# A causal linear attention feeding a snake feed-forward layer on one core: a rebuilt head, another planner, shifted preferences

## The chip, the core and the metric

The kernel runs on one core of a Trainium2 chip. A core has a matrix engine (PE; its weight loads are shown apart as PEld), a vector engine (DVE), a scalar engine (ACT), a general engine (POOL) and a queue engine (SP) that issues most transfers. Each takes its instructions in order and waits on semaphores. PE multiplies tiles of up to 128 x 128 weights by up to 512 columns and writes into eight accumulator banks; DVE and ACT read these banks, POOL does not. Transfers issued by SP, ACT and POOL are moved by the same 16 DMA engines.

The metric is the device time of one execution in microseconds (us); less is better. The profile is one execution taken by the hardware profiler, and its span runs from the first to the last recorded instruction.

## The reference, cut to what matters

```python
for b in range(nb):                    # 12 blocks of 64 positions; B=4, H=8, S=768, D=64
    intra = einsum('bhic,bhjc->bhij', qb, kb) * Dmask      # lam**(i-j) for i >= j
    intra = einsum('bhij,bhjd->bhid', intra, vb)
    inter = einsum('bhid,bhde->bhie', qb * lam_pow, kv_state)
    out[:, :, sl] = intra + inter
    kv_state = lam_block * kv_state + einsum('bhsd,bhse->bhde', kb * rev_pow, vb)
x = out.transpose(0, 2, 1, 3).reshape(3072, 512)
h = x @ w_in                           # 512 x 2048
g = h + sin(alpha * h)**2 / (alpha + 1e-09)
return g @ w_out                       # 2048 x 512
```

An attention whose weights decay by lam per position, then a feed-forward layer with the function h + sin^2(alpha h)/alpha.

## The kernel before, in words

**Tiling.** The kernel takes 24 blocks of 128 positions (6 per batch entry, numbered s = 0 to 23) and groups four of them into a chunk of 512 rows, six chunks in all. Per block, `scale_block` multiplies q by powers of lam and k by inverse powers (POOL, some on DVE in the first four blocks) and casts v (ACT or POOL). `piece_T`, `piece_Q` and `piece_K` transpose the scaled q and k through PE for blocks below 12 (a DMA transpose does it from block 12 on) and copy the result into `qkT`. `part_S` multiplies k by q into two banks; DVE multiplies them by the mask into `Sm` (L646). `part_Z` adds k times v into bank 7, the running state, which is copied into `Zd` (block diagonal, L681) or `Zc` (L686). `part_O` adds the part from the state (`Zd` or `Zc` times q, L708 or L721) and the part within the block (v times `Sm`, L730) in one bank, and its `then` copies that bank, transposed x, into `xT` (L740).

Per chunk c and slice m of 128 of the 2048 hidden columns, `unit_A` multiplies w_in by `xT` (4 matmuls of 512 columns, L779), ACT takes the sine (L789), POOL or ACT squares it (L794 or L793), DVE forms `gT` from it and the bank (L796). `unit_A2` does two slices for half a chunk (8 matmuls of 256 columns, L813; L823, L827 or L828, L831). `unit_B` multiplies `gT` by w_out for 128 rows and four slices (4 matmuls, L844); after four of them ACT copies the bank into `osb` (L857) and it is stored (L859).

**The first four blocks (the head).** q of blocks 0 to 3 is loaded so that a partition holds four neighbouring positions, so a bank of outputs holds, for each t of 4, the positions 4x+t; the copy at L740 writes them in natural order, with a step of four elements of two bytes. Before its first real work PE multiplies a constant tile (`spin`, L935). A column block of 512 of w_in is loaded as f32 into `ws` and cast by DVE (L415); the rest of w_in and all of w_out are loaded with a cast by POOL's queue.

**What sets the order.** The program lists operations with what they read and write; `_Plan` orders them. It keeps a clock per engine, takes a duration from each `op` call, and places the operation that can start first; where several can start within a slack the one listed first goes (minus its `lead`). ACT, DVE and POOL operations are free in order, and an operation with a list of engines goes to the one that would end it first by these costs. PE may look 40 operations ahead, SP stays in listed order. Transfers are planned as an issue, a fixed 0.8 us, their duration shared among queues, and a latency. The result is a fixed instruction order with semaphore waits; the chip does not choose again.

```python
    AHEAD = {"PE": 40, "SP": 1}
    SLACK = 0.3
    LAT = 0.2
```

Of the kernel before, what the change touches and what calls it, by code (L numbers as in the profile page):

```python
# [32 lines left out]
class _Plan:  # L33

    AHEAD = {"PE": 40, "SP": 1}
    SLACK = 0.3  # L40
    EARLY = 0.0, 0.0

    LAT = 0.2
# [10 lines left out]
    def op(self, eng, emit, dur, reads=(), writes=(), dma=None, after=(), issue=0.4, lat=2.6, runs=64):  # L54
# [14 lines left out]
        o.deps.discard(o)  # L69
        o.lead = self.lead  # L70
# [4 lines left out]
    def _transfers(order):  # L75
# [5 lines left out]
        left = {e: [[o.start + 0.8, o.runs, o.dur / o.runs, o] for o in sorted(q, key=lambda o: o.start)]  # L81
# [19 lines left out]
    def _settle(self):  # L101

        filler, lands, best = self.filler, {}, None
        for _ in range(8):
            self.filler = filler
            for o in self.ops:
                o.eng, o.start, o.done = o.given, None, None
            order = self._order(lands)
            new = self._transfers(order)
            off = sum(abs(t - o.done) for o, t in new.items())  # L110
            state = [(o, o.eng, o.start, o.done) for o in order]
            if best is None or off < best[0]:
                best = off, order, state
# [5 lines left out]
    def _order(self, lands):  # L119
        index = {o: i - o.lead for i, o in enumerate(self.ops)}  # L120
        left = {}
        for o in self.ops:
            left.setdefault(o.eng if isinstance(o.eng, str) else "any", []).append(o)
        fixed = {e: left.pop(e, []) for e in ("PE", "SP")}
        free = [o for e in left for o in left[e]]
        clock = {e: 0.8 for e in ("PE", "SP", "ACT", "DVE", "POOL")}
        wire = 0.0
        port = 0.0
        order = []

        def ready(o):
            t = 0.0
            for d in o.deps:
                if d.done is None:
                    return None
                t = max(t, d.done + (0.0 if d.eng == o.eng else self.LAT))
            return t

        while fixed["PE"] or fixed["SP"] or free:
            best = None  # L140
            for e in ("PE", "SP"):
                can = []
                for o in fixed[e][:self.AHEAD[e]]:
                    r = ready(o)
                    if r is not None:
                        can.append((max(r, clock[e]), index[o], o, e, o.dur))
                if can:
                    soon = min(c[0] for c in can)
                    soon += self.EARLY[1] if e == "PE" and soon < self.EARLY[0] else self.SLACK
                    c = min((c for c in can if c[0] <= soon), key=lambda c: c[1])  # L150
                    if best is None or c[:2] < best[:2]:
                        best = c
            for o in free:
                r = ready(o)
                if r is None:
                    continue
                if o.port:
                    r = max(r, port)
                if isinstance(o.eng, str):
                    c = (max(r, clock[o.eng]), index[o], o, o.eng, o.dur)  # L160
                else:
                    _, e, d = min((max(r, clock[e]) + d + late, e, d) for e, d, late in o.eng)
# [81 lines left out]
def bass_lightning_attn__then__act_snake_kernel(  # L244
# [24 lines left out]
    R2 = 6  # L269
# [766 lines left out]
```

## Time and profile before

| | us |
|---|---|
| runs of the kernel before | 224.34, 221.33, 223.85; median 223.85 |
| profiled execution | 221.06, of which the span is 219.2 |
| PE busy | 207.6 (95% of the span) |
| ACT busy | 157.2 (72%) |
| DVE busy | 123.0 (56%) |
| POOL busy | 96.0 (44%) |
| first matmul of the feed-forward (L813) | starts at 20.58 |
| last matmul (L844) | ends at 216.6 |

Between the profiled execution's time and its span lie 1.86 us. A line of the timeline has the start in us, the duration in us, the engine (with q, its instruction queue), the line of the code, the operation, the tile written and the tile read, the shape and the number of instructions merged; in brackets the idle time of the engine just before and what ended it. A line of the chain of work that ended last has a start, a duration and what ran. A line of the waits has who waited for whom, the total in us, the number of times and the longest. PE durations include a modelled end, so that neighbouring ones overlap; starts are the better measure. Some matmul records are missing: where a group of four shows as x3 with 0.16 us of "issue" before it, the gap is one missing matmul.

### The profile page before, as it was taken

What the parts mean: (1) busy time and instruction counts of PE and PEld (TensorE: products, weight loads), DVE (VectorE), ACT (ScalarE), POOL (GpSimd) and SP (SyncE); (2) the same over time, 40 slices, a digit from 0 to 9 for tenths busy, and PEclk for the clock granted to TensorE, in tenths of its full rate; (3) what the DMA queues carried; (4) which work ended last, traced back from release to release, by engine and by line L of the source; (5) the groups of instructions that cost most, each with busy time, mean ns of one, the idle gap of its engine ahead of it and who ended that gap; (6) DMA issues with size and microseconds to landing.
All of it is one profiled execution on the core that took longest, in us unless ns stands there. A gap on an engine that the chain in (4) does not pass through costs nothing.

```text
span 219.2 us, 4238 instructions
## 1 busy us (share of the span) xinstructions
PE 207.6 (95%) x1714; PEld 112.2 (51%) x1739; DVE 123.0 (56%) x185; ACT 157.2 (72%) x279; POOL 96.0 (44%) x110
## 2 busy tenths in 40 slices
PE   7787999999999979999999999999999999999995
PEld 2365544446577656555445444545544444444454
DVE  4688675444878858957564556545464544444100
ACT  4577986364988888969798787878778677777221
POOL 7793677756886777574551533011001011110100
PEclk9999999999999999999999999999999999999999
DMA  4999999999999999999999560110011011101212
GB/s 132 310 314 210 207 215 214 220 219 250 235 314 221 240 186 271 162 290 179 281 254 208 123 144 10 41 48 35 16 48 51 0 48 48 51 0 48 87 58 96
DMA packets 78499, 33.31 MB, mean 152 GB/s; under 512 B 55296, under 2 KB 75536, under 8 KB 78480
## 3 DMA queue, kind: packets, MB, share of 16 engines
q1 hardware_dynamic: 71728, 24.25, 53.4%
q0 software_dynamic: 3696, 3.67, 10.1%
q10 hardware_dynamic: 3056, 5.13, 6.5%
q8 instruction: 13, 0.21, 0.4%
q14 instruction: 6, 0.05, 0.1%
HBM read 27.28 MB, written 6.29 MB: 153 GB/s over the span
## 4 chain that ended last, share of the span: by engine, by line
PE 66%; DMA 20%; POOL 5%; ACT 3%; DVE 2%; issue 2%; SPq 1%; ACTq 0%; POOLq 0%
PE bank L844 33%; PE bank L779 22%; DMA k<-in_k_dram 10%; PE bank L813 4%; DMA w<-in_moe_w_in_dram 4%; DMA q<-in_q_dram 3%; DMA v<-in_v_dram 3%; PE bank L730 2%; PE bank L635 2%; POOL qk L513 2%; SPq L346 1%; POOL u L794 1%; POOL qk L505 1%; PE bank L708 1%; DVE gT L831 1%
## 5 line engine op out<-in xcount | busy, mean ns | idle before, releaser
L844 PE MATMUL bank<-w,gT 128*128 128x512 bf16 (+1 forms) x382 | 91.3, 371 | 1.8 <-issue 1.3
L796 DVE SCALAR_TENSOR_TENSOR gT<-u,rinv,bank 128x512 bf16<-128x512 bf16 x74 | 54.6, 745 | 52.2 <-ACT u L793 30.0
L779 PE MATMUL bank<-xT,w 128*128 128x512 bf16 x290 | 73.1, 379 | 0.6 <-issue 0.2
L789 ACT ACTIVATE t<-bank,alpha 128x512 bf16<-128x512 f32 x74 | 50.5, 686 | 23.2 <-PE bank L779 23.1
L794 POOL TENSOR_TENSOR u<-t 128x512 bf16<-128x512 bf16 x26 | 26.9, 1039 | 86.6 <-ACT t L789 84.7
L844 PEld LDWEIGHTS bank<-w,gT 128*128 128x128 bf16 x400 | 37.9, 98 | 39.5
L779 PEld LDWEIGHTS bank<-xT,w 128*128 128x128 bf16 x296 | 28.5, 98 | 34.1 <-ACT xT L740 0.6
L646 DVE TENSOR_TENSOR Sm<-bank,mask 128x1024 bf16<-128x1024 f32 x24 | 29.1, 1222 | 10.4 <-PE bank L671 7.1
L793 ACT ACTIVATE u<-t 128x512 bf16<-128x512 bf16 x48 | 30.0, 628 | 1.3
L857 ACT COPY osb<-bank 128x512 f32<-128x512 f32 (+1 forms) x25 | 14.2, 571 | 14.3 <-PE bank L844 14.2
L505 POOL TENSOR_TENSOR qk<-q,Lq 128x512 bf16<-128x512 f32 x20 | 20.4, 1042 | 8.2 <-DMA q<-in_q_dram 8.2
L813 PE MATMUL bank<-xT,w 128*128 128x256 bf16 x176 | 22.5, 273 | 1.5 <-DVE gT L831 1.5
L525 POOL TENSOR_TENSOR qk<-k,Lk 128x512 bf16<-128x512 f32 x20 | 20.8, 1042 | 2.6 <-DMA k<-in_k_dram 2.5
L823 ACT ACTIVATE t<-bank,alpha 128x256 bf16<-128x256 f32 x44 | 18.5, 474 | 4.5 <-PE bank L813 4.1
L831 DVE SCALAR_TENSOR_TENSOR gT<-u,rinv,bank 128x256 bf16<-128x256 bf16 x44 | 18.8, 474 | 4.9 <-ACT u L827 2.6
L813 PEld LDWEIGHTS bank<-xT,w 128*128 128x128 bf16 x176 | 16.1, 98 | 4.8 <-DVE gT L831 2.4
L740 ACT CAST xT<-bank 128x512 bf16<-128x512 f32 (+1 forms) x18 | 14.4, 799 | 3.6 <-PE bank L671 2.2
L528 ACT CAST v<-v 128x512 bf16<-128x512 f32 x16 | 9.8, 614 | 4.3 <-DMA v<-in_v_dram 4.3
L828 POOL TENSOR_TENSOR u<-t 128x512 bf16<-128x512 bf16 x9 | 9.3, 1038 | 6.5 <-ACT t L823 6.5
L730 PE MATMUL bank<-Sm,v 128*64 128x128 bf16 (+1 forms) x224 | 11.0, 224 | 0.6 <-DVE Sm L646 0.3
L635 PE MATMUL bank<-qkT 64*128 64x128 bf16 (+1 forms) x224 | 9.6, 219 | 0.3 <-ACT qkT L594 0.2
L935 PE MATMUL bank<-idle 128*128 128x512 bf16 x21 | 8.4, 540 | 1.6 <-DVE idle L441 1.5
(68 smaller groups left out, 125.7 us busy)
## 6 DMA issues: line engine op xcount, KB each, us to landing
q<-in_q_dram SPq DMA_DIRECT2D x12, 512.0 KB, 5.6
k<-in_k_dram SPq DMA_DIRECT2D x24, 256.0 KB, 5.5
v<-in_v_dram SPq DMA_DIRECT2D x24, 256.0 KB, 5.7
out_dram<-osb ACTq DMA_DIRECT2D x19, 256.0 KB, 2.0
w<-in_moe_w_out_dram POOLq DMA_DIRECT2D x4, 512.0 KB, 12.7
w<-in_moe_w_in_dram POOLq DMA_DIRECT2D x3, 512.0 KB, 8.0
ws<-in_moe_w_in_dram SPq DMA_DIRECT2D x2, 512.0 KB, 6.2
out_dram<-osb SPq DMA_DIRECT2D x4, 256.0 KB, 4.2
```

Of the source, the lines that this page charges most:

```text
L505: lambda e, a=a: e.tensor_tensor(qk2[:, j:j + 2, 4 * a:4 * a + 4, :], q32[:, jq, 4 * a:4 * a + 4, :, :].rearrange("p h t d -> p t h d"), b ...
L525: lambda e: e.tensor_tensor(qk2[:, j, H:2 * H, :], block32(k32, jl), lk, ALU.mult), 1.05,
L646: op("DVE", lambda e: e.tensor_tensor(Sm[js][:, :, :], banks[:, 512 * b0:512 * b0 + 1024].rearrange("p (c i) -> p c i", i=128), bass.AP(ma ...
L779: ins = e.matmul(ps[hb][:, c0:c1], w1[:, kc, 128 * m:128 * (m + 1)], xT[x][:, kc, c0:c1], start=(kc == 0 and c0 == lo), stop=(kc == NKC - ...
L789: op("ACT", lambda e: e.activation(t16[ju][:, w], ps[hb][:, w], ACTF.Sin, scale=alpha[:, m:m + 1]), 0.69 * f, [bank(hb), "alpha"], [("t16" ...
L793: lambda e: (e.activation(u16[ju][:, w], t16[ju][:, w], ACTF.Square) if e is nc.scalar else e.tensor_tensor(u16[ju][:, w], t16[ju][:, w], ...
L794: e.tensor_tensor(u16[ju][:, w], t16[ju][:, w], t16[ju][:, w], ALU.mult)), 0,
L796: op("DVE", lambda e: e.scalar_tensor_tensor(out=gT[g][:, m, w], in0=u16[ju][:, w], scalar=rinv[:, m:m + 1], in1=ps[hb][:, w], op0=ALU.mul ...
L813: ins = e.matmul(ps[hb][:, 256 * i:256 * i + 256], w1[:, kc, 128 * (m + i):128 * (m + i + 1)], xT[x][:, kc, lo:lo + 256], start=(kc == 0 a ...
L823: op("ACT", lambda e, i=i: e.activation(t16[ju][:, 256 * i:256 * i + 256], ps[hb][:, 256 * i:256 * i + 256], ACTF.Sin, scale=alpha[:, m + ...
L831: op("DVE", lambda e, i=i: e.scalar_tensor_tensor(out=gT[g][:, m + i, lo:lo + 256], in0=u16[ju][:, 256 * i:256 * i + 256], scalar=rinv[:, ...
L844: ins = e.matmul(ps[ob][:, w], gT[g][:, m, 128 * s4:128 * (s4 + 1)], w2[:, m, w], start=(m == 0), stop=(m == NM - 1),)
```

## The change

1. **Head, constants.** The decay rates `lam` are loaded by SP ahead of q instead of by ACT. An Exp of one element stands right behind the Ln. The copy of alpha moves to ACT, behind the load of the Sin table; the two small DVE operations on it are listed later.
2. **Head, scaling.** All four q operations and three of four k operations of blocks 0 to 3 go to DVE (before: two q and one k), the rest to POOL; they are marked so that the planner does not lay DVE's and POOL's over each other. v: one of four on ACT.
3. **Head, transposes and outputs.** `piece_Q` can use two banks, with one ACT copy for each half. `piece_P` computes the part within the block for two blocks at once, each 64 x 64 matmul in one of four quarters of the array (32 matmuls for two blocks; before 16 for each block in turn); `piece_I` adds the part from the state. `evict` copies to `xT` with a step of two elements instead of four, all but half of the last block on ACT.
4. **First rows.** The rows of chunk 0 are now in another order in `xT`, so each group of 128 rows goes out in two stores of 64 partitions (eight stores on SP instead of four).
5. **Planner.** Every engine may take the earliest in preference among the operations that can start within a window (0.3 us for PE, 0.1 for ACT, DVE and POOL). A clock is freed a little before an operation's result is ready (`PIPE`), a hand-over costs `HOP` (plus `DRAIN` behind PE), transfers start 2.0 us after their issue (2.9 for POOL). Durations are changed all over. SP follows preferences too.
6. **Twelve shifts.** `MOVES` adds to the preference of stretches of operations.
7. The filler matmuls have 256 columns instead of 512.

In the built program ACT has 82 squares (before 61) and POOL 14 (before 35); ACT has 24 copies to `Zd` (before 19), DVE 2 (before 7). The counts of feed-forward matmuls are equal. SP loads k of one of blocks 4 and 5 ahead of q of the pair; on POOL's queue the first two loads of w_out stand ahead of the last load of w_in.

```diff
-    AHEAD = {"PE": 40, "SP": 1}
-    SLACK = 0.3
-    EARLY = 0.0, 0.0
-    LAT = 0.2
+    AHEAD = 40
+    WINDOW = {"PE": 0.3, "ACT": 0.1, "DVE": 0.1, "POOL": 0.1}
+    PIPE = {"ACT": 0.11, "DVE": 0.09, "POOL": 0.045, "PE": 0.0}
+    HOP = {"PE": 0.055, "ACT": 0.035, "DVE": 0.035, "POOL": 0.075, "SP": 0.1}
+    DRAIN = 0.085
+    MOVES = (
+        (112, 1, "SP", -15), (532, 3, "SP", -15), (291, 1, "all", 20), (104, 1, "all", 35),
+        (194, 30, "all", 35), (255, 10, "all", 50), (315, 1, "all", -110), (349, 30, "DVE", 125),
+        (487, 1, "all", -25), (80, 30, "all", -5), (328, 10, "SP", -20), (346, 3, "DVE", 740),
+    )
+    SPIN = 0.22, 0.11, 7.4
...
+        self.lag = 2.9 if eng == "POOL" else 2.0
...
     def _settle(self):
...
+        prio = {o: i - o.lead for i, o in enumerate(self.ops)}
+        for at, width, kind, by in self.MOVES:
+            for o in self.ops[at:at + width]:
+                if (kind == "all" and o.given != "SP") or o.given == kind or (kind == "any" and not isinstance(o.given, str)):
+                    prio[o] += by
...
+                soon = min(x[0] for x in c) + self.WINDOW.get(e, 0.0)
+                x = min((x for x in c if x[0] <= soon), key=lambda x: (x[1], num[x[2]]))
+                if best is None or x[0] < best[0]:
+                    best = x[0], x[2], e, x[3]
...
+                o.done = t + dur
+                clock[e] = o.done - self.PIPE[e]
...
-    QD = ((0, 0), (1, 0))
+    QD = ((0, 0), (0, 2), (1, 0), (1, 2))
...
-            load(lam_bc[:, :], bass.AP(lam.tensor, 0, [[0, 128], [1, H]]), "lam", 0.1, "lam", "ACT", runs=1)
+            load(lam_bc[:, :], bass.AP(lam.tensor, 0, [[0, 128], [1, H]]), "lam", 0.1, "lam", "SP", lat=0.8, runs=1)
...
+            op("ACT", lambda e: e.activation(warm[:, :], lnlam[:, 0:1], ACTF.Exp, scale=0.0), 1.5, ["lnlam"], ["warm"])
...
-            op("DVE", lambda e: e.tensor_copy(alpha[:, :], ps[4][:, 0:NM]), 0.2, [bank(4)], ["alpha"])
+            op("ACT", lambda e: e.copy(alpha[:, :], ps[4][:, 0:NM]), 0.2, [bank(4), "warm"], ["alpha"])
...
-                        eng, dur = (("DVE", 0.9) if a == 0 else ("POOL", 1.05)) if s == 0 else ("POOL", 1.05)
-                        (op(eng, lambda e, a=a: e.tensor_tensor(
+                        eng, dur = ("DVE", 0.68) if s + a < 3 else ("POOL", 1.05)
+                        ported(op(eng, lambda e, a=a: e.tensor_tensor(
...
+            def evict(s, obs):
+                jq, nq, u = queries(s)
+                c, i4 = s // BPC, s % BPC
+                P.lead = -20
+                for eng, a0, a1, dur in (("ACT", 0, 2, 0.46), ("DVE", 2, 4, 0.4)) if len(obs) > 1 else (("ACT", 0, 4, 0.74),):
+                    op(eng, lambda e, a0=a0, a1=a1: (e.copy if e is nc.scalar else e.tensor_copy)(
+                        xT[c % RX][:, a0:a1, BL * i4:BL * (i4 + 1)].rearrange("p a (u x t) -> p a u t x", u=nq // 2, t=2),
...
+            def piece_P(s, *obs):
...
+                    for t in range(2):
+                        for jp in range(4):
+                            for h in range(2):
+                                for i in range(2):
+                                    r = slice(64 * i, 64 * i + 64)
+                                    ins = e.matmul(
+                                        ps[obs[i][jp // 2]][64 * h:64 * h + 64, 128 * jp:128 * (jp + 1)],
+                                        v2[r, j + t, 2 * jp + h, :], Sm[sm[t]][r, 4 * h + jp, :],
...
+            def piece_I(s, *obs):
+                jq, nq, u = queries(s)
...
+                            Zd[(s - 1) % 2][:, jp, :], qkT[:, jq:jq + nq, jp, u],
...
-                    op(eng, lambda e: e.dma_start(out[row:row + 128, w], osb[jo][:, w]), 0.75,
-                       [("osb", jo)], [], dma=f"out{jo}", issue=0.3, runs=8)
+                    for u in range(1 if c else 2):
+                        rows = out[row:row + 128, w] if c else bass.AP(
+                            out.tensor, (row + 2 * u) * DM + lo, [[4 * DM, 32], [DM, 2], [1, hi - lo]])
+                        got = osb[jo][:, w] if c else osb[jo][64 * u:64 * u + 64, w]
...
             piece_S(2, 1, 2)
             piece_Z(0)
-            piece_O(0, 3)
             piece_S(3, 5, 6)
+            piece_P(0, 3, 4)
             piece_Z(1)
-            piece_O(1, 4)
+            piece_I(1, 4)
             piece_Z(2)
-            piece_O(2, 1)
-            piece_O(3, 2, 5)
+            piece_P(2, 1, (2, 5))
+            piece_I(2, 1)
+            piece_I(3, 2, 5)
...
-                    ins = e.matmul(ps[0][:, :], idle[:, 0:128], idle[:, :])
+                    ins = e.matmul(ps[0][:, 0:256], idle[:, 0:128], idle[:, :])
```

More of the change, by code (lines that the diff above doesn't have):

```diff
@@ L69, in op @@
         o.deps.discard(o)
+        if lag is not None:
+            o.lag = lag
         o.lead = self.lead
@@ L101, in _settle @@
     def _settle(self):
[L103 to L111, printed above, removed]
+        prio = {o: i - o.lead for i, o in enumerate(self.ops)}
[3 more added lines that the diff above has]
+                    prio[o] += by
+        lands, best = {}, None
+        for _ in range(10):
+            order, new, off = self._pass(prio, lands)
             if best is None or off < best[0]:
-                best = off, order, state
+                best = off, order, [(o, o.eng, o.start, o.done) for o in order]
+            if off < 0.5:
+                break
             lands = new
@@ L117, in _settle, with _pass @@
         return best[1]
[L119 to L121 removed]
+    def _pass(self, prio, lands):
         for o in self.ops:
[L123 to L168 removed]
@@ L194, in _order @@
             order.append(o)
+            can.discard(o)
+            left -= 1
+            for s in after.get(o, ()):
+                waits[s] -= 1
+                if not waits[s]:
+                    can.add(s)
         return order
@@ L595, in piece_K, with run @@
                        0.6, [bank(tbs[t])], [("kT", jt + t)])
-            def run(*parts, after=()):
+            def run(*parts, after=(), lead_then=-20):
                 parts = [p for p in parts if p is not None]
```

238 lines of the change are left out of this document (161 added, 77 removed).

## The prediction

> **What bounds the kernel now.** I read the page's slices first: PE is at 0.9 or more of its time in nearly all of the 40, and the matrix clock is granted in full throughout. So the time is the start of PE's real work, plus that work, plus its stalls. The timeline of the head shows when the work starts:
>
> ```profile
> 15.79 1.31 ACT L740 CAST xT<-bank 128x512 bf16<-128x512 f32 x1 [0.23 <-PE bank L730]
> 16.83 0.86 ACT L681 CAST Zd<-bank 64x256 bf16<-64x256 f32 x2
> 17.71 1.32 ACT L740 CAST xT<-bank 128x512 bf16<-128x512 f32 x1
> 18.77 0.86 ACT L681 CAST Zd<-bank 64x256 bf16<-64x256 f32 x2
> ...
> 20.58 2.02 PE L813 MATMUL bank<-xT,w 128*128 128x256 bf16 x16
> ...
> 22.65 1.68 PE L779 MATMUL bank<-xT,w 128*128 128x512 bf16 x7
> ```
>
> ACT alternates between copies of the state and of x without a pause; the last parts of xT come from it, and the first matmul of full width starts at 22.65. DVE is as full from 12.71: four Sm of 1.155 each, then the casts of ws:
>
> ```profile
> 9.52 1.52 DVE L513 TENSOR_TENSOR qk<-k,Lp 128x512 bf16<-128x512 f32 x1
> ...
> 12.71 4.62 DVE L646 TENSOR_TENSOR Sm<-bank,mask 128x1024 bf16<-128x1024 f32 x4 [0.53 <-PE bank L635]
> 17.24 1.79 DVE L415 CAST w<-ws 128x1024 bf16<-128x1024 f32 x2
> ```
>
> Then the waits of PE after the head, from the list of waits; "issue" entries are missing records, not waits:
>
> ```profile
> PE bank L813 <- DVE gT L831: 1.5, 2, 1.2
> ...
> PE bank L543 <- POOL qk L525: 0.5, 1, 0.5
> ```
>
> That is about 2.2 us with the small ones: all that a planner can win in the 196 us from 20.58 to the last matmul at 216.6. The chain of the work that ended last tells where the 0.48 (at 41.27) and the 1.20 (at 79.71) come from:
>
> ```profile
> 23.92 16.09 DMA k<-in_k_dram
> 40.08 1.05 POOL qk L525
> ...
> 71.40 6.17 DMA v<-in_v_dram
> 77.60 0.62 ACT v L528
> 78.21 0.54 ACT u L827
> 78.78 0.88 DVE gT L831 x2
> 79.71 1.05 PE bank L813 x8
> ```
>
> A load of k competes with the weights for 16 us; and an ACT queue stands behind a cast whose v has not landed, with the square that PE's bank needs behind it.
>
> **The head, step by step.** *Transfers.* lam ahead of q on SP costs one issue (0.46), so q starts at 1.27 instead of 0.81 and all that follows on that queue is 0.46 later. The second k landed at 9.19 (2.42 + 6.77); at some 290 GB/s a load of 262 KB takes 0.9, so the four k land at 8.7, 9.65, 10.55, 11.45, the four v at 12.35 to 15.05, and ws (10.13 + 6.0 and 11.0 + 6.5 before) at 16.6 and 18.0.
>
> *Constants.* lam took 3.5 from issue; at worst it lands at 4.3 again, at best with the 1.7 of a small store, 2.5. The dummy Exp saves nothing: the table load for Exp already started at 4.59, right behind the Ln, ahead of the DVE product at 4.61; it adds 0.2. Even with the late lam the factors are there at 6.2, and q lands at 1.27 + 5.0 (the shortest of its rows) = 6.3. Before, scaling began at 6.15: what is late next is q, so this step is worth nothing.
>
> *DVE.* Four q at 0.66: 6.3 to 8.95. k: to 9.6, 10.3; the small operation 0.6, to 10.9; third k to 11.6. Here I take 0.66, the row for q, not the 1.52 of the one k row, which ran beside POOL's k; only the third now meets POOL, so the bound is +0.85. Copy of k 0.42, reciprocal 0.25: Sm can begin at 12.3 and ends at 16.9 (before 17.33). The first cast of ws ends at 17.8.
>
> *POOL* has one k (11.45 to 12.5) and v to 13.85, then issues two weight loads until 15.5, fourth v to 16.1. The first weight load is issued at 13.85 instead of 13.45.
>
> *ACT.* k copies to 14.1, v 0.62 to 14.8. Then Zd 0.76, x, Zd 0.86, x, Zd 0.76, x and half an x. What is x worth? The step-4 copies took 1.31, half of one 0.73; later blocks with step 2 take 0.72 to 0.74 (L740 at 139.26, for one). I take 0.74 and 0.45: x ends at 16.3, 17.85, 19.4 and the half at 19.85. The matmuls hide beside it: the pair product waits for the last Sm (16.9) and the third state, runs 17.6 to 18.25 (before 0.47 of weight loads per 16, so 0.94 for 32 as an upper bound), the state part follows to 18.6, the last one to 19.05.
>
> [...]
>
> *Sum.* PE's first eight half-width matmuls 19.05 to 19.9, the next eight from 19.9 to 20.8 (second ws cast done at 20.55), first full-width matmul at 20.8 against 22.65: **1.85 won**. Bounds: 0.8, if DVE's k are slow and ws is held up by the earlier weight loads; 2.5, if lam's transfer hides and the Zd copies run at the 0.36 of the later rows.
>
> **From 20.8 to 42.** The loads do not move, as DMA is full from 4 to 40 us. k of the pair follows q as before, so the transpose that waited until 41.27 comes at about 41.6 (the weights start 0.4 later). But three more units of the output layer (3 x 0.863 = 2.6) are now ordered ahead of it, so PE reaches it at 20.8 + 0.44 + 14 x 0.863 + 9 x 0.863 + 0.45 = 41.55: the 1.85 is filled and the 0.48 goes. Net 2.6 - 0.3 = 2.3 ahead. Those units need the third load of w_out at about 38.5; it was issued at 24.57, and these loads took 12.7 (median) to 15.0, so it lands between 37.3 and 39.6: a wait of 0 to 1.1, I take 0.3 by the median. **2.0 won by 42.**
>
> **After 42.** Planned time to landing of a v goes from 4.5 (0.8 + 1.1 + 2.7) to 5.9 (2.0 + 1.18 + 2.7); the rows say 5.5 to 5.7, and 6.17 in the stall shown. Costs of ACT and DVE also move toward the rows (square 0.6 to 0.63 against 0.628). So I expect half of the 1.46 at L813 gone, **0.75**; bounds 1.46 and a loss (below). The eight stores instead of four hold SP longer (four took 2.83 from 59.39, so up to 2.8 more), and k and v of block 13 stand behind them. The cover: before, q of that pair was issued at 62.26, transposed from 73.09 on, and used by PE from 85.86, where a DMA transpose takes 5.4 to land: some 4 us to spare. I cost it at nothing; without that cover, up to 2. The tail (last matmul to end) stays at 2.6.
>
> **Sum.** 219.2 - 2.0 - 0.75 = 216.45, and with 1.86 around the span **218.3**, against the profiled 221.06 (-1.2%). The three runs have a median of 223.85, 1.3% above that execution: two executions lie near 221.2 (the profiled one with them), two near 224.1. The same two levels for the changed kernel would be 218.3 and 221.2. I forecast **219.4**, a third of the way up. About 2% is what a measurement of this kernel can tell from no change.
>
> **Rivals.**
> - *Everything works:* head 2.5 and all 2.2 of stalls gone: 214.5 + 1.86 = 216.4, 2.1% faster. For it: the costs match the rows now. Against: loads still decide at 40. Chance 0.20.
> - *The head's gain is waited away:* the third and fourth w_out loads, now behind another order, land a microsecond or two later (the fourth is issued only when the last of w_in, moved behind two others, has landed). PE waits at 38 to 42, and only the 0.75 stays: 218.45 + 1.86 = 220.3. Chance 0.16.
> - [...] Chance 0.10. [...]
> - *ACT becomes the bound (slower):* 21 squares move from POOL (1.04) to ACT (0.53 start to start before an independent one), with 5 Zd copies. From 86 to 130 ACT was busy 36.5 of 44, with 6 store issues of 0.34 besides; six to eight squares more and some copies make about 44. There is then no room, and each late v holds PE's banks as at 79.71, for 1.2. It decides from about six such waits on: 6 x 1.2 over the forecast, 225.5, 2% slower. Against: the new plan counts ACT's time closely, and POOL was open to it at a cost. Chance 0.10.
>
> The forecast's own case has 0.44. The range runs from 216.4 to 220.3 + 2.9 = 223.2; beyond it lie the slower case and an upper tail. Faster by over 2%: the first rival and a part of the forecast at its low level, 0.29; slower by over 2%: 0.09; within: 0.62.
>
> **What would show it.** x copies of 0.74 on ACT in the head; Sm from about 12.3; the first full-width L870 near 20.8; no wait of DVE on ACT above 1 us around 60 to 80; ACT near 172 us busy in all. Wrong if L870 starts after 22, if PE waits over 1 us for a w_out load near 38, or if PE's waits on DVE's gT grow past 2.

## The result, and the profile after

The changed kernel took 219.28 us (median of four runs, 218.18 to 221.55) against 222.97 for the kernel before beside it (four runs, 221.33 to 224.34): a ratio of 0.985, 95% interval 0.980 to 0.990. It is faster, by less than the 2% that separates a change from none. The ratio is of the means of all four runs; without the one of 221.55, which lies over 1.5% above the fastest and so counts as a slow run, it is 0.982. The forecast was 219.4, with a range of 216.4 to 223.2.

The profile after is of the slowest of the four runs: 221.55, with a span of 219.8, 0.6 longer than the span of before. One trace thus shows both what was won and where it was lost again. On its page, the slices of PE and of the granted clock:

```profile
PE   7788999999999998959999999999999999999995
...
PEclk9999999999999999979999999999999999999999
```

A slice is 5.5 us. In the 16th and the 18th (82 to 88 and 93 to 99) PE waits, and the 18th shows a clock of 0.7. Before, the slice with a wait was the 15th, and none showed a lower clock. The timeline of the head, for DVE, ACT and PE (start, busy time, engine and line, and in brackets the idle time ahead of it):

```profile
3.74 0.21 ACT L486 ACTIVATE lnlam<-lam_bc 128x8 f32<-128x8 f32 x1 [1.20 <-DMA lam_bc<-in_lam_dram]
3.96 1.28 ACT L488 ACT_TABLE_LOAD   x1
...
5.61 2.66 DVE L519 TENSOR_TENSOR qk<-q,Lq 128x512 bf16<-128x512 f32 x4 [1.07 <-ACT Lq L491]
...
11.10 4.64 DVE L680 TENSOR_TENSOR Sm<-bank,mask 128x1024 bf16<-128x1024 f32 x4 [0.22 <-PE bank L669]
...
14.61 0.73 ACT L787 CAST xT<-bank 128x512 bf16<-128x512 f32 x1
...
17.34 0.32 PE L705 MATMUL bank<-v,qk 64*64 64x64 bf16 x9 [1.12 <-issue]
...
18.83 1.91 PE L904 MATMUL bank<-xT,w 128*128 128x256 bf16 x16
20.79 1.67 PE L870 MATMUL bank<-xT,w 128*128 128x512 bf16 x7
```

Scaling starts at 5.61 (before 6.15), Sm at 11.10 (12.71), a copy of x takes 0.73 (1.31), and the first recorded full-width matmul starts at 20.79 (22.65). In between PE stops for 1.12 at a place where the profile shows nothing that it waits for: two of the sixteen small matmuls of that group stand before the gap and fourteen behind it, and no semaphore is waited on inside a group. Next, the stretch from 88 to 101, the instructions of PE, the DMA transposes of SP and a store of ACT:

```profile
89.08 1.99 SPq L558 DMA_TRANSPOSE qkT<-qk  x1
...
90.63 0.34 ACTq L954 DMA_DIRECT2D out_dram<-osb  x1
...
92.74 1.03 PE L935 MATMUL bank<-w,gT 128*128 128x512 bf16 x4
...
95.90 0.38 PE L742 MATMUL bank<-qkT,Zd 128*128 128x128 bf16 x4 [2.13 <-issue]
...
97.73 2.79 PE L870 MATMUL bank<-xT,w 128*128 128x512 bf16 x7 [0.33 <-issue]
100.36 0.81 PE L935 MATMUL bank<-w,gT 128*128 128x512 bf16 x3
```

L742 is the first reader of the block that the transpose of 89.08 brings, and that transpose landed 6.7 after its issue, at 95.8. So I read this "issue" of 2.13 as a wait for it. Behind it seven full-width matmuls take 2.79 where seven in the head took 1.67: the array is at a lower rate. The windows of four microseconds say by how much (length, busy time of PE, of its weight loads, DVE, ACT and POOL, then the granted clock):

```profile
92.00:96.00 4.00, 1.87 (x11) 0.72 (x9) 2.15 (x3) 2.25 (x4) 2.02 (x2) 1.00 1.18 204
96.00:100.00 4.00, 3.67 (x34) 2.07 (x34) 1.65 (x2) 1.71 (x4) 2.52 (x3) 0.57 1.63 206
```

At 0.57, 4 us do the work of 2.28: 1.72 lost, besides the wait. Cut finer, it is one stretch at 0.50, from 96.57 to 99.98. PE's list of waits, first rows:

```profile
PE bank L742 <- issue: 2.1, 1, 2.1
...
PE bank L705 <- issue: 1.1, 1, 1.1
PE bank L935 <- issue: 1.1, 7, 0.2
PE bank L669 <- DMA qkT<-qk: 0.8, 1, 0.8
```

The row of before for L813 on DVE's gT (1.5) has no successor: that wait is gone. L935, seven times up to 0.2, is missing records. The chain of waits that the prediction followed to 40.08 and 77.60 now runs over ACT near 40 (from 35.93 to 41.70, the last of it a copy of the transposed q) and over a DMA transpose near 79.

### The profile page after: what moved, and what is told of

Read it like the earlier page. It is cut to its first block, busy times and chain, and to the rows that moved or that the text cites. A ratio compares the mean times of both kernels' runs of the same rounds, so it can differ in the third digit from the quotient of the medians.

```text
span 219.8 us, 4312 instructions
## 1 busy us (share of the span) xinstructions
PE 207.7 (94%) x1747; PEld 115.1 (52%) x1771; DVE 118.7 (54%) x181; ACT 168.4 (77%) x311; POOL 69.3 (32%) x85
## 4 chain that ended last, share of the span: by engine, by line
PE 81%; ACT 8%; DMA 5%; issue 3%; SPq 1%; POOL 0%; POOLq 0%
PE bank L935 35%; PE bank L870 28%; PE bank L904 7%; PE bank L764 3%; DMA k<-in_k_dram 3%; PE bank L669 3%; DMA qkT<-qk 3%; ACT t L880 1%; SPq L372 1%; ACT u L884 1%; PE bank L705 1%; PE bank L742 1%; PE bank L568 1%; ACT t L914 1%; ACT Zd L715 1%
## 5 line engine op out<-in xcount | busy, mean ns | idle before, releaser
L935 PE MATMUL bank<-w,gT 128*128 128x512 bf16 (+1 forms) x382 | 91.6, 370 | 1.7 <-issue 1.1
L870 PE MATMUL bank<-xT,w 128*128 128x512 bf16 x290 | 74.3, 384 | 0.6 <-issue 0.3
L935 PEld LDWEIGHTS bank<-w,gT 128*128 128x128 bf16 x400 | 37.8, 98 | 39.4
L870 PEld LDWEIGHTS bank<-xT,w 128*128 128x128 bf16 x296 | 29.0, 99 | 35.2 <-issue 1.7
L884 ACT ACTIVATE u<-t 128x512 bf16<-128x512 bf16 x67 | 42.1, 629 | 2.0
L549 POOL TENSOR_TENSOR qk<-k,Lk 128x512 bf16<-128x512 f32 x20 | 20.8, 1042 | 9.9 <-DMA k<-in_k_dram 9.8
L904 PE MATMUL bank<-xT,w 128*128 128x256 bf16 x176 | 21.9, 273 | 0.0
L904 PEld LDWEIGHTS bank<-xT,w 128*128 128x128 bf16 x176 | 16.2, 98 | 2.6 <-DVE gT L922 0.2
L919 POOL TENSOR_TENSOR u<-t 128x512 bf16<-128x512 bf16 x7 | 7.3, 1038 | 15.7 <-ACT t L914 15.7
L715 ACT CAST Zd<-bank 64x256 bf16<-64x256 f32 x24 | 8.7, 362 | 4.0 <-PE bank L705 3.7
L1034 PE MATMUL bank<-idle 128*128 128x256 bf16 x54 | 9.1, 313 | 1.3 <-DVE idle L467 1.3
L774 ACT CAST xT<-bank 128x512 bf16<-128x512 f32 x14 | 10.2, 728 | 0.0
L918 ACT ACTIVATE u<-t 128x512 bf16<-128x512 bf16 x15 | 9.5, 636 | 0.3
```

Of the source, the lines that this page charges most:

```text
L549: lambda e: e.tensor_tensor(qk2[:, j, H:2 * H, :], block32(k32, jl), lk, ALU.mult), 1.05,
L870: ins = e.matmul(ps[hb][:, c0:c1], w1[:, kc, 128 * m:128 * (m + 1)], xT[x][:, kc, c0:c1], start=(kc == 0 and c0 == lo), stop=(kc == NKC - ...
L884: lambda e: (e.activation(u16[ju][:, w], t16[ju][:, w], ACTF.Square) if e is nc.scalar else e.tensor_tensor(u16[ju][:, w], t16[ju][:, w], ...
L904: ins = e.matmul(ps[hb][:, 256 * i:256 * i + 256], w1[:, kc, 128 * (m + i):128 * (m + i + 1)], xT[x][:, kc, lo:lo + 256], start=(kc == 0 a ...
L935: ins = e.matmul(ps[ob][:, w], gT[g][:, m, 128 * s4:128 * (s4 + 1)], w2[:, m, w], start=(m == 0), stop=(m == NM - 1),)
```

## The experiments

Twelve runs were made, four at a time on one chip, each beside the kernel before; two of them are the changed kernel itself. Where an edit is not to change the order of the work, the list that the planner made for the changed kernel is kept and only the named operations are dropped, moved or given another engine.

### Which part carries the gain

**The planner's shifts.** All twelve left out, everything else as changed:

```diff
-    MOVES = (
-        (112, 1, "SP", -15), (532, 3, "SP", -15), (291, 1, "all", 20), (104, 1, "all", 35),
-        (194, 30, "all", 35), (255, 10, "all", 50), (315, 1, "all", -110), (349, 30, "DVE", 125),
-        (487, 1, "all", -25), (80, 30, "all", -5), (328, 10, "SP", -20), (346, 3, "DVE", 740),
-    )
+    MOVES = ()
```

> The changed kernel without the twelve shifts of preference; planner and head as changed, so the order differs in all engines. Theory (small): the new planner's costs do the work and the shifts win at most 1 us; 0 to 1 us slower. Rival (shifts carry it): without them stalls of PE come back near 40 or near 85, 1.5 to 4 us slower, about the kernel before.

Measured: 225.35 (223.76 to 225.94) beside 224.98 for the kernel before, ratio 1.001 (0.996 to 1.006). The head is that of the changed kernel (first full-width matmul at 20.54), and the end is that of before. Its waits and the place, from the list of waits and the timeline of PE:

```profile
PE bank L665 <- DMA qkT<-qk: 4.0, 1, 4.0
```

```profile
87.22 0.61 PE L665 MATMUL bank<-qkT 64*128 64x128 bf16 x8 [3.96 <-DMA qkT<-qk]
```

A wait of 4.0 for the transpose issued at 80.30, and a clock of 0.50 from 87.06 to 90.47: half of 3.41 is up to 1.7 more. The rival holds: the shifts carry the gain. So two microseconds won in the head are worth nothing if PE then stands at a transpose.

**Three shifts on SP, or nine on the engines.** First the three alone, then the nine alone:

```diff
     MOVES = (
-        ... twelve
+        (112, 1, "SP", -15), (532, 3, "SP", -15), (328, 10, "SP", -20),
     )
```

> The twelve shifts are cut to the three that move DMAs on SP (one load of k, one DMA transpose, three loads of a pair). Theory (what matters is that the transposes and loads of 75 to 97 are issued earlier): at least half of the gain of the twelve, 222 or less, the wait of PE for the DMA transposes (4.0 without shifts) down to 2 or less, no slice at half rate there. Rival (the nine shifts on the engines carry it, by filling PE in 52 to 86): 224.5 to 225.5 as without shifts, with the wait of 4.

Measured: 222.44 (221.47 to 225.73, ten runs) beside 222.53, ratio 0.9995 (0.995 to 1.004). The theory falls, although the wait for transposes fell to 0.9 in the trace as it said: PE was busy 31.97 of the 34 us from 52 to 86, and waited 1.2 for Sm instead. The rival's wait of 4 did not come back either, and its 224.5 to 225.5 was taken from another chip; by the ratio the time is that of no shifts (1.001).

```diff
     MOVES = (
-        ... twelve
+        (291, 1, "all", 20), (104, 1, "all", 35), (194, 30, "all", 35), (255, 10, "all", 50),
+        (315, 1, "all", -110), (349, 30, "DVE", 125), (487, 1, "all", -25), (80, 30, "all", -5),
+        (346, 3, "DVE", 740),
     )
```

> The other nine of the twelve shifts, those of engine work, without the three of SP's DMAs (which alone left the time at that of the kernel before). Theory (the nine let PE run fuller in 52 to 86, where it was busy 30.1 of 34 without shifts and 33.0 with all, and the transposes of 75 to 97 are then the limit): a gain of 1 to 2 us on the kernel before, PE 32.5 or more of 34 in 52 to 86, a PE wait of 2 or more on a transpose after 80. Rival 1 (only all twelve together help): the time of the kernel before within 1. Rival 2 (the three SP shifts add nothing): the time of the changed kernel beside it within 0.7.

Measured: 219.0 (218.66 to 220.43) beside 218.8 for the changed kernel on the same chip and 223.79 for the kernel before, ratio 0.983 (0.974 to 0.992). Rival 2: the three shifts on SP add nothing that can be measured; the nine on the engines carry the gain. The trace shows how: the wait of 4.0 is now

```profile
84.63 0.40 PE L667 MATMUL bank<-qkT 64*128 64x128 bf16 x8 [0.35 <-DMA qkT<-qk]
```

PE comes 1.0 later to that place (84.3, against 83.3 without shifts, with other work done before it), the transpose is issued at 78.90 instead of 80.30, and it lands after 5.7 instead of 6.9. The theory asked for a wait of 2 or more on a transpose after 80; the longest is 0.5.

**Planner and head one by one.** The kernel before with the new planner class (its lists of costs are those of before), without shifts:

```diff
-class _Plan:   # of the kernel before
+class _Plan:   # of the changed kernel, MOVES = ()
...
-            P.EARLY = 20.0, 0.3
```

> The kernel before with the new planner class in place of the old, without its shifts; head, stores and copies are those of before. Theory (the planner by itself brings nothing, the shifts do): within 2 us of the kernel before, a little above it, 222 to 227, with a wait of 3 us or more on a DMA transpose in 80 to 97. Rival (the planner is the gain): under 220.

Measured: 228.92 (228.05 to 229.46) beside 222.53, ratio 1.027 (1.019 to 1.034): about 6 us slower, more than either theory said, and not by the wait on a transpose that was expected: its first full-width matmul comes at 27.59, 4.9 later than before, so most of it is lost in the head. It is no clean measure of the planner, though. The planner counts 0.22 and later 0.11 for a filler, which fits 256 columns, and the fillers of this kernel have 512. It laid 58 of them in the head, 15.9 of PE's time (21 recorded and 8.4 in the kernel before), and the first transposes came at 11.53 instead of 8.19. Then the other half, the new head under the planner of before:

```diff
-class _Plan:   # of the changed kernel
+class _Plan:   # of the kernel before
...
+            P.EARLY = 20.0, 0.3
```

> The changed head with all operations and durations as changed, ordered by the planner of the kernel before (no shifts). Theory (head first): the first full-width matmul comes 1.5 us or more earlier than before (22.65), and the time lies 1 to 2 us under the kernel before, 0.7 to 1.5 over the changed one. Rival (planner): the old planner gives the head's gain back in waits, the time is that of the kernel before within 0.7.

Measured: 228.02 (226.34 to 230.45) beside 224.98, ratio 1.011 (1.006 to 1.017). This pair is mismatched the other way: the planner of before counts 0.4 for a filler, and here a filler has half the columns. In its trace, of the slowest of the four runs, PE stands for 2.97 in the head and 4.0 ahead of 89.05, and the clock is 0.50 from 20.23 to 23.65 and from 88.50 to 95.33. So neither part was a gain in these two pairings; what each is worth with fillers and costs that fit it is not shown. Both together without the shifts are no gain, and all three together are 1.0 to 1.9%.

### The copies, and what the head is worth

The copies at a step of four come back, and the order of columns with them; the half stores take 64 rows in a row instead of every other pair:

```diff
-   xT[...].rearrange("p a (u x t) -> p a u t x", u=nq // 2, t=2),
+   xT[...].rearrange("p a (x t) -> p a t x", t=nq),
...
-   out.tensor, (row + 2 * u) * DM + lo, [[4 * DM, 32], [DM, 2], [1, hi - lo]])
+   out[row + 64 * u:row + 64 * u + 64, w]
```

> The changed kernel with its order kept, only the copies to xT of blocks 0 to 3 write natural order with a step of four elements again (each 128-row group still goes out in two stores, of 64 neighbouring rows). Theory (rows): the three full copies on ACT take 1.31 instead of 0.73 and the halves 0.73 instead of 0.45, ACT's chain carries two to three of them, so the first full-width matmul comes 1.2 to 1.9 us later and the time grows by 1 to 2. Rival (hidden): the pause of PE at 16.2 to 17.3 or the second half of ws sets the start of the real work, and the time grows by less than 0.5. [...]

Measured: 218.39 (217.89 to 218.68) beside 224.98, ratio 0.971 (0.968 to 0.974). The copies cost what they cost before, from the timeline of ACT:

```profile
14.65 1.31 ACT L787 CAST xT<-bank 128x512 bf16<-128x512 f32 x1
...
16.58 1.29 ACT L787 CAST xT<-bank 128x512 bf16<-128x512 f32 x1
```

and the first full-width matmul comes at 21.44, where the changed kernel's second trace, also with all eight records, has 20.51. So the head is 0.9 later, not the 1.2 to 1.9 of the theory, and the end is earlier: the wait at L742 is not there. This was on another chip than the first measurement, so it ran again beside the changed kernel.

> The kernel with the plain copies and the half stores in the order of the rows once more, beside the changed kernel on one chip. Theory (it was faster because PE, 1 us later, also brings ACT's store 1 us later, so that the transpose lands after 4.4 and the wait at 94 is gone): 1 to 3 us less than the changed kernel beside it, no PE wait over 1 us after 86. Rival (the two were on different chips, and the plain copies cost their 0.7 at the first full-width matmul): 0.5 to 1 us more.

> The changed kernel beside the next three on one chip. Its two profiles so far show PE waiting at 93.4 to 96.3 for the DMA transpose issued at 89.1, which lands 6.7 and 7.0 after its issue, and a store of 256 KB issued by ACT at 90.5, between the two. Theory and rival expect the same of it: that wait again, between 2 and 3 us, and 218 to 222.5.

Measured: 218.46 (217.92 to 218.76) with the old copies, 218.8 (218.69 to 219.19) for the changed kernel, and 223.79 for the kernel before, ratios 0.979 (0.972 to 0.986) and 0.981 (0.974 to 0.988). The two can't be told apart. The expectation for the changed kernel was wrong, and its trace tells more for that. It has neither the wait nor the low clock near 96, but one in the head:

```profile
17.49 0.32 PE L705 MATMUL bank<-v,qk 64*64 64x64 bf16 x9 [1.33 <-issue]
19.08 3.47 PE L904 MATMUL bank<-xT,w 128*128 128x256 bf16 x16
22.60 0.59 PE L870 MATMUL bank<-xT,w 128*128 128x512 bf16 x2
```

The sixteen half-width matmuls took 3.47 instead of 1.91, and full width begins at 22.60, where it began before the change (22.65). The head's whole gain is missing in this execution, and it ended at 218.81, 2.7 earlier than the one that had it.

### The place where PE stops in the head

In eleven traces PE stopped behind its 221st matmul: in ten of the changed kernel and its variants between 16.0 and 17.6, for 0.57 to 1.34, and under the planner of before at 17.2, for 2.97 (in the kernel before it is 0.23, behind the 220th):

```profile
20.21 0.52 PE L680 MATMUL bank<-v,qk 64*64 64x64 bf16 x11 [2.97 <-issue]
```

To see whether the place or the time decides, each filler of 256 columns became two of 128:

```diff
-                for _ in range(n):
-                    ins = e.matmul(ps[0][:, 0:256], idle[:, 0:128], idle[:, :])
+                for _ in range(2 * n):
+                    ins = e.matmul(ps[0][:, 0:128], idle[:, 0:128], idle[:, 0:128])
```

> Each filler matmul of the head is replaced by two of half its width, in the same places; nothing else moves. Four traces show PE pausing, with no releaser in sight, in front of one and the same matmul, the 222nd of the program. Theory (the pause belongs to the place in the program, as when its next instructions have to be brought in): with twice the fillers the 222nd matmul is in the first group L807, which starts at 13.6; the pause shows there, the group at 16.0 runs through, L904 starts at about 17.7 instead of 18.8, and L870 about 1.1 earlier, at 19.5. Rival (the pause belongs to the time or to the data of that group): PE pauses again at 16.0 to 17.3 and L870 starts at 20.6. For the end, theory A (the head's gain is carried through, so 1.1 earlier at L870 is 1.1 at the end): about 1 us less than the changed kernel beside it. Theory B (what the head gains is waited away in the stretch from 52 to 97, as in the kernel without shifts, whose head was the same and whose end was that of the kernel before): within 0.5 of it.

```profile
13.60 0.55 PE L807 MATMUL bank<-Sm,v 64*64 64x128 bf16 x25
15.02 0.30 PE L807 MATMUL bank<-Sm,v 64*64 64x128 bf16 x7 [0.87 <-issue]
```

The pause is now inside L807, behind matmul 222, and the group at 16 runs through. It belongs to the place in the program. On the size of the gain the expectation was wrong: PE then waits for others, and the first full-width matmul comes at 20.12, 0.4 earlier and not 1.1. The time was 220.32 (219.05 to 221.31) against 221.18 (219.41 to 222.68) for the changed kernel beside it, ratios to before of 0.988 (0.980 to 0.996) and 0.990 (0.979 to 1.001): nothing is told by that of theory A or B.

What brings the instructions in is seen only from outside: the DMA queue of instructions moved 14 packets of 0.23 MB in all, one of them in 14 to 15 us of the changed kernel, in 16 to 17 of before and in 17 to 18 under the old planner, some 3 us before PE went on each time, while the DMA engines were full (0.9 or more in the DMA slices from 11 to 22 of both pages). That the pauses of 0.57 to 2.97 are a wait for such a packet is argued from the place and the packet's time, not shown.

### The stores and the transposes

The eight stores of the first rows on ACT instead of SP, the order of everything kept:

```diff
-                        op(eng, lambda e, rows=rows, got=got: e.dma_start(rows, got), ...)
+                        o = op(eng, lambda e, rows=rows, got=got: e.dma_start(rows, got), ...)
+                        if not c:
+                            P.moved[o] = "ACT"
```

> The changed kernel with its order kept, only the eight stores of chunk 0 are issued by ACT instead of SP. In the changed kernel's profile SP spends 8.7 us on these stores between 60 and 70, the first four DMA transposes are issued at 74.5, 78.9, 85.2 and 89.1 (before the change 73.1, 77.7, 82.9, 87.3), and PE waits 0.75 at 84.6 and 2.13 at 95.9 for transposed blocks, then runs at half rate for about 4 us. Theory (stores): they hold the loads behind them, so the transposes move 1.5 to 4 us earlier, both waits and the half rate go, 3 to 4 us against that profiled execution and 1 to 3 in the timed ratio. Rival (pace): the loads behind are held by buffers that come free late, not by the stores; the transposes stay within 0.5 us and the time within 0.5. Second rival (ACT): eight issues of 0.35 on a full ACT cost PE waits on gT of 1 us or more between 60 and 75.

Measured: 218.95 (218.86 to 220.62) beside 224.98, ratio 0.975 (0.971 to 0.980). The transposes are issued 1.1 to 2.1 earlier than in the profile after (four rows: 72.37, 77.84, 83.31 and 87.62 against 74.47, 78.90, 85.24 and 89.08), PE waits for none, and the clock is full. In their place PE waits once for ACT, 1.32 at 59.94 for `Zc`, a price of the kind that the second rival feared. I took the earlier transposes for the cause. The kernel beside it with the old copies spoke against it: there the stores are on SP still, the transposes are issued at 74.32 to 89.58, PE waits 0.9 for the one of 78.81, and not at all at L742. Its transpose of 89.58 landed after 4.4.

So the question was what makes that one transpose land after 6.7 at one time and 4.4 at another. The changed kernel once more, for a second trace:

> The changed kernel once more, beside the three others on one chip, for the comparison. Theory (the eight stores delay the DMA transposes, and what that costs differs from execution to execution, through the half-rate stretch that follows a PE wait of about 2 us): its times spread over 218 to 221.5, and where its trace shows no half-rate slice near 97, it has no PE wait near 2 us there either. Rival (the half-rate stretch of the first profile was chance and has nothing to do with the stores): times within 0.5 of each other, no other cause to be seen.

Measured: 221.18 (219.41 to 222.68). Transpose issued at 89.21, landed after 7.0, PE waits 2.73, and the clock is 0.75 and 0.82 in the two windows of 4 us behind it (one stretch at 0.50, from 98.00 to 101.41). With the halved fillers, beside it on the same chip, the transpose of 89.63 took 6.3 and PE waited 2.47, but the clock stayed full:

```profile
96.00:100.00 4.00, 3.94 (x42) 2.19 (x43) 2.02 (x3) 2.69 (x5) 2.36 (x3) 1.00 1.31 238
```

and that trace's span is 218.4, against 220.3. In these three ACT had issued a store of 256 KB 0.8 to 1.55 behind the transpose; with the old copies it was 2.05 behind it, and with the stores on ACT 4.2. So that one store was moved, behind the fifth instruction of ACT that followed it:

```diff
         order = self._settle()
+        store, behind = self.ops[497], self.ops[478]
+        order.remove(store)
+        order.insert(order.index(behind) + 1, store)
```

> The changed kernel with one instruction moved: the store of 256 KB that ACT issues at 90.6 is put five instructions later on ACT, behind the u of 93.7, so that it is issued at about 94. Theory (that store, in the engines beside the DMA transpose of 89.1, is what makes the transpose land after 6.7 instead of 4.4): the transpose lands in 5.2 or less, the wait of PE in front of L742 falls from 2.1 to 2.7 down to under 0.8, no half-rate stretch follows, and the time is 1.5 to 3 us under that of the changed kernel beside it, near 217.5 to 218.5. Rival 1 (the loads of k and v that SP issues at 87.8 and 88.5 make the transpose late, or a wait that is not on the transpose ends at 96): the wait stays at 2 or more and the time within 0.5. Rival 2 (the transpose of 95.3 meets the store instead): the wait moves to the next use of a transpose, and the time stays within 1.

From the timeline (line numbers are three higher here):

```profile
87.85 2.25 SPq L561 DMA_TRANSPOSE qkT<-qk  x1
...
92.06 1.03 PE L938 MATMUL bank<-w,gT 128*128 128x512 bf16 x4
...
92.92 0.39 PE L745 MATMUL bank<-qkT,Zd 128*128 128x128 bf16 x4
92.99 0.36 ACTq L957 DMA_DIRECT2D out_dram<-osb  x1
```

The transpose landed after 4.6, PE does not wait, and the profiled execution took 217.28, the shortest of all. But the four runs are 217.28, 217.84, 219.16 and 220.3, median 218.5, against 218.8 beside it, ratio 0.980 (0.972 to 0.989): not told apart. And the changed kernel itself, beside it on that chip, had a transpose of 4.5 with the store 2.3 behind it, so the moved store has nothing to be set against. The nine traces fit together:

| trace | store behind the transpose of 87 to 90 | landed after | PE's wait at L742 |
|---|---|---|---|
| halved fillers | 0.8 | 6.3 | 2.5 |
| changed, second trace | 1.3 | 7.0 | 2.7 |
| changed, first trace | 1.55 | 6.7 | 2.1 |
| old copies, first | 2.05 | 4.4 | none |
| changed, third trace | 2.3 | 4.5 | none |
| nine shifts | 2.8 | 4.4 | 0.5 |
| old copies, second | 3.5 | 4.4 | none |
| stores on ACT | 4.2 | 4.4 | none |
| store moved | 5.1 | 4.6 | none |

That a store close behind makes the transpose late fits these nine and stays short of shown. For it: the kernels without shifts, with the three on SP, and the two mixed ones have the store of that fourth transpose 4.4 to 9.6 behind, and it lands after 4.3 to 4.5. The second transpose (issued at 77 to 82) landed after 5.7 to 7.3 in the seven traces with a store 0.2 to 1.8 behind it, and after 4.4 and 3.1 in the kernel before and with the stores on ACT, where none came within 2. And the loads of k and v ahead of the fourth stand alike in long and short (87.83 and 88.45 in the first trace, 88.11 and 88.73 in the third), so they are not the difference. Against it: the kernel before has a transpose of 5.9 (issued 87.27) with its store 5.8 behind, and in the first trace the one issued at 95.32 took 6.7 with no store behind it until 104.99. The runs without a profile may have had other waits.

## Why the prediction was right

Time and verdict came out as forecast, and several steps behind them did not. That 219.4 met 219.28 so closely is in part luck: a third of the way from 218.3 to 221.2 was a guess.

- **lam on SP, "this step is worth nothing": wrong.** Scaling waited for Lq (1.07, the row at 5.61), not for q. q was there before 5.61, although I let it land at 6.3 by the shortest of its rows; lam landed sooner, so that Ln ran at 3.74 instead of 4.36. Scaling started 0.54 earlier than before. The step was not undone by itself; the rows of the two heads show it.
- **The dummy Exp saves nothing: right.** The table load stands right behind the Ln at 3.96, as at 4.59 before, and the operation costs 0.20 on ACT.
- **DVE's scalings at 0.66 to 0.69: right** (2.66 for four, 1.29 for two). Sm started at 11.10, not 12.3: 0.7 from lam, and 0.5 from the third k and the small operations.
- **The copies of x at 0.74: right** (0.73 at a step of two, and 1.31 at a step of four with the old order back). Both are now measured on ACT in one head.
- **First full-width matmul at 20.8: right by two errors.** Sm came 1.2 sooner, and PE stopped for 1.12 at matmul 221, which I had not seen: in the trace of before that pause is 0.23 and I read it as a missing record.
- **20 to 42: the time right, the wait another.** The transpose on PE comes at 41.76 (41.55 to 41.6 forecast), waits 0.24 and not 0.48, and no wait for w_out is in the trace. But the load of k no longer sets it: POOL scaled the two k of the pair at 28.51 and 38.48 (40.08 and 42.41 before), and the 0.24 is for ACT's copy of the transposed q (L600, 40.69 to 41.70). The second rival, that the head's gain is waited away, had its outcome right for that one execution and its mechanism and place wrong: the gain was lost at 94, at a transpose and the low clock behind it, not at 38 to 42 for w_out, and the time, 221.55, is above the 220.3 it gave.
- **After 42, "half of the 1.46 gone, 0.75": mis-sized.** The whole wait is gone, and more. PE's idle time from 42 to 165 was 3.48 before. In two traces of the last four runs, both without a wait at L742, the changed kernel and the one with the moved store, it is 2.0 and 1.8 (with about as many missing records): 1.5 to 1.7 won, the upper bound and a little more.
- **"The eight stores cost nothing, without the cover up to 2": the step that failed in the profiled execution.** The stores held SP for 8.7, not for the 2.83 + 2.8 that I allowed. The transposes of 73 to 87 came 1.2 to 2.4 later, and the cover of 4 us was not there: PE waited 0.75 and 2.13 for two of them, and the array ran at 0.50 for 3.41 us behind the second. Yet the stores are only one of the things that use the cover up, since five traces with the stores on SP have no wait at L742, or one of 0.5.
- **ACT as the bound: did not happen.** ACT was busy 168.4 (172 forecast), and no wait of DVE for ACT from 58 to 86 exceeds 0.58.

The terms add up. Against the trace of before (span 219.2, full width at 22.65, PE idle 4.11 in 22 to 165), in traces with equally many missing records:

| trace | head | PE idle, 22 to 165 | low clock after 22 | sum | span |
|---|---|---|---|---|---|
| changed, first | -1.86 | 5.02: +0.91 | +1.72 | +0.8 | 219.8: +0.6 |
| changed, third | -0.05 | 2.17: -1.94 | +0.1 | -1.9 | 216.9: -2.3 |
| store moved | -1.71 | 2.12: -1.99 | none | -3.7 | 215.2: -4.0 |

So the head's gain does reach the end where nothing waits at the transposes; in one execution it was lost there, and in another it never came about, with the array at 0.50 in 20 to 22. The forecast span of 216.45 lies between. The third trace also shows that a sign of the prediction was too strict: full width after 22 was to mean that it is wrong, and that execution took 218.81. It is also the one of the changed kernel's three traces in which the array was at half rate when the real work started (0.50 from 18.86 to 22.27, some 1.7 us), right behind the pause.

The rise to 219.4 I took from the two levels of the kernel before, without a cause. A cause that is now seen is a wait or a pause after which the array runs at half rate for 3.41 us, which costs 1.7, at places that differ from run to run. The mean granted clocks of the thirteen runs of the kernel before that stood beside the second four go with it: one such stretch in 220 us makes a mean of 0.992, and the five runs at 0.992 took 221.75 to 222.41, the three at 0.984 or 0.985 took 222.53 to 223.11, the three at 0.977 took 224.15 to 224.85. Two at 1.000 took 221.5 and 223.94, so it is not all.

Why was the same pause of 1.33 at matmul 221 followed by a low clock in the changed kernel's third trace and not with the store moved? In every trace that records a change of the clock, these times lie whole multiples of 3.413 us apart (27, 1 and 35 of them in the first trace, 62 in that of before; the last change, at the end, is among them). So the trace can be cut into stretches of that length, beginning at its first change. The two that matter, and the ones behind them, first in the third trace and then with the store moved:

```profile
15.44:18.86 3.42, 1.85 (x58) 1.23 (x56) 0.98 (x2) 2.03 (x6) 2.02 (x3) 1.00 1.22 263
18.86:22.27 3.41, 3.41 (x19) 2.42 (x18) 1.02 (x2) 2.11 (x5) 0.00 (x0) 0.50 1.24 208
...
15.08:18.49 3.41, 1.92 (x60) 1.44 (x58) 1.34 (x2) 2.05 (x6) 2.38 (x4) 1.00 1.19 273
18.49:21.90 3.41, 3.29 (x29) 2.35 (x28) 1.34 (x3) 3.06 (x8) 0.00 (x0) 1.00 1.24 209
```

The pause lay a little differently in the two stretches, and PE was busy for 1.85 in one and 1.92 in the other. All thirteen traces that record a change agree in this. Up to 205 us they have 732 such stretches at full clock; the six in which PE was busy for 1.85 or less (0.00, 0.00, 0.44, 1.29, 1.67, 1.85) are each followed by 0.50, and the 726 with 1.92 or more by full clock. That is read off these traces; nothing was changed to test it, and busy time is partly modelled.

What stays open: what makes the transpose late in one execution and not in another, and what head and planner are worth apart.

## What to carry to other kernels

When PE is near full, look past the stage that is sped up to the next transfer that PE meets just in time: without the shifts, 2 us won in the head were all given back at one DMA transpose and in the half-rate stretch behind it. A cover read from one execution needs the spread of the transfer's landing beside it (here 4.4 to 7.0 for the same transpose). An "issue" wait in the middle of a group of PE, or longer than a missing record, is to be counted and compared between kernels by the number of the matmul, before it is set aside.

## What the hardware did that was not expected

- The low clock came in stretches of 3.41 us at 0.50 (once two in a row), whatever the wait was: a wait of 2.13, one of 2.73, one of 4.0 and a pause of 1.33 were each followed by one, which costs 1.7. A wait of 2.47 was followed by none: it fell across two stretches, in which PE was busy for 2.06 and 2.29. PE was not idle throughout ahead of each: in three of the six stretches that were followed by a low clock it was busy for 1.29 to 1.85 us.
- PE stops with no releaser in sight at a fixed number of matmuls (220 to 222) for 0.2 to 2.97 us while the DMA engines are full (0.9 or more in the DMA slices from 11 to 22 of the pages before and after); that it waits for its own instructions is argued, not shown.
